# Order of query loads and DMA transposes in one DMA queue, and of the weight formation, in a fused attention and feed-forward kernel

## Chip, cores, metric

One core of one Trainium2 chip. The metric is the device time of one execution in microseconds (us). A run is one execution; every run also lists the mean clock that TensorE was granted, as a share of its full speed.

## The reference

A linear attention (softmax of q over the head dimension, softmax of k over the sequence, two small products) feeds a feed-forward stage.

```python
# q, k, v: (8, 8, 576, 64)   w1, w2: (512, 1024)   w3: (1024, 1024)   w_out: (1024, 512)
q_s = softmax(q, axis=-1);  k_s = softmax(k, axis=2)
kv   = einsum('bhsd,bhse->bhde', k_s, v)
attn = einsum('bhsd,bhde->bhse', q_s, kv)
x    = attn.transpose(0, 2, 1, 3).reshape(4608, 512)
out  = (((x @ w1) * (x @ w2)) @ w3) @ w_out
```

## The kernel before

The kernel folds w3 and w_out into one matrix W3O (the "weight formation"), so that the feed-forward stage is, for each of nine chunks of 512 tokens, a first stage (`s1`, products with w1 and w2) and a second stage (`s2`, product with W3O). The attention of batches 2 to 8 is woven in between. Batches are counted from one in this text; in the code the index is one less.

The parts that matter: every load, DMA transpose (`DMA_TRANSPOSE` in the traces) and output store but the very last is issued by SyncE into one queue, in program order. A query batch goes load, exponential (ScalarE, `eq`), sums (VectorE, `ds`), normalisation (GpSimd, `eqn`), transpose by DMA (`qsT`), product (TensorE, tile `att`), copy to `xT`.

```python
stage = ctx.enter_context(tc.tile_pool(name="stage", bufs=12))   # every load lands here
...
def load_qkv(b, which, i):
    t = slot([P, 2, R * D])                                      # 576 KB
    nc.sync.dma_start(out=t, in_=...)
def dma_t(b, i):
    nc.sync.dma_start_transpose(out=qt_tile(b, i), in_=eqns[(b, i)].rearrange("p r h d -> p (r h d)"))
...
LOADS = [("q", 0), ("q", 1), ("k", 0), ("v", 0), ("k", 1), ("v", 1)]
...
    exp_k(1, 1, 1)
    dma_t(1, 0)                     # second batch's transposes ...
    dma_t(1, 1)
    for which, i in LOADS:          # ... ahead of the third batch's loads
        load_qkv(2, which, i)
...
def step():                         # one step of the attention between two matmul blocks (cut)
    ...
    if b == 2 and n == 9:
        for m in range(6):          # all six loads of the fifth batch, one in each step
            due.setdefault(t + 1 + m, []).append(lambda m=m: load_qkv(4, *LOADS[m]))
    ...
    if n in (2, 5):
        due.setdefault(t + 3, []).append(lambda: dma_t(b, n // 3))
```

In the traces of before and after, the DMAs of the queue name eight completion semaphores in turn, and of the 145 DMAs with an eighth one ahead of them none was issued before that one had landed: the query load issued at 66.06 in the trace of before is the eighth after the key load issued at 55.23, which landed at 66.05. The recorded texts call this queue the ring, and count on landings in the order of issue: in both traces all 154 DMAs landed so.

The softmax here doesn't subtract the row's maximum and nothing guards it: scores larger than these inputs give would overflow.

## Time and profile before

| | before |
|---|---|
| median of 4 runs | 253.57 us (252.31 to 255.34) |
| profiled span | 253.0 us, granted clock 0.986 |
| TensorE (PE) busy | 238.8 us, 94% |

The page of the profile, first its busy line and then three rows of its slices (40 equal slices of 6.3 us; the digit is the busy share in tenths):

```profile
PE 238.8 (94%) x1405; PEld 114.2 (45%) x1405; DVE 129.2 (51%) x235; ACT 110.9 (44%) x190; POOL 66.8 (26%) x63
...
PE   8989999997969978999999999999999999999993
...
PEclk9999999999997997999999999999999999999999
DMA  7999999789899999999799651451111132112335
```

TensorE is full from slice 17 to slice 39; slice 40 is the end. Its weak slices are 10, 12, 15 and 16; the clock is down in the slices 13 and 16, each time with or right after a weak one; and up to there the DMA engines are nearly full, with a shallow hole in slices 8 to 11. The prediction shows the single gaps.

### The profile page before, as it was taken

The numbers are of one execution on the slowest core, as the hardware profiler recorded it, in microseconds if no ns is written. First come the engines' busy times: TensorE is split into PE (matmuls) and PEld (weight loads), VectorE is DVE, ScalarE is ACT, GpSimd is POOL, SyncE is SP. The second block draws the span as 40 slices with busy tenths as digits, with TensorE's granted clock in tenths as the row PEclk, the third lists the DMA queues.
The fourth block names the chain that finished last, engine by engine and source line by source line (L and its number), as shares of the span: only waits on it lengthen the run. The fifth ranks groups of instructions, "written<-read, shape, count | busy, mean of one in ns | idle before, by whom it ended". The sixth has DMA issues, their size and how long they took to land.

```text
span 253.0 us, 3872 instructions
## 1 busy us (share of the span) xinstructions
PE 238.8 (94%) x1405; PEld 114.2 (45%) x1405; DVE 129.2 (51%) x235; ACT 110.9 (44%) x190; POOL 66.8 (26%) x63
## 2 busy tenths in 40 slices
PE   8989999997969978999999999999999999999993
PEld 2534545453424433454454445445444444444442
DVE  2668544757565372546547647635344343444342
ACT  4578515717537615645645563743411222122200
POOL 3655842613621611603503413420000000000000
PEclk9999999999997997999999999999999999999999
DMA  7999999789899999999799651451111132112335
GB/s 243 385 348 367 398 404 391 267 209 383 270 233 373 391 307 374 333 317 396 136 225 370 92 103 39 96 115 41 44 41 41 41 78 49 43 41 58 68 78 131
DMA packets 41875, 52.62 MB, mean 208 GB/s; under 512 B 18816, under 2 KB 22912, under 8 KB 41856
## 3 DMA queue, kind: packets, MB, share of 16 engines
q1 hardware_dynamic: 41776, 52.24, 68.8%
q8 instruction: 11, 0.18, 0.3%
q10 hardware_dynamic: 80, 0.13, 0.1%
q14 instruction: 8, 0.07, 0.1%
HBM read 38.80 MB, written 9.44 MB: 191 GB/s over the span
## 4 chain that ended last, share of the span: by engine, by line
PE 67%; DMA 24%; SPq 4%; DVE 1%; issue 1%; ACT 1%; POOL 0%
PE pab L218 39%; PE po L261 20%; DMA qsT<-eqn 7%; DMA st<-in_moe_w_out_dram 4%; DMA st<-in_k_dram 4%; DMA st<-in_q_dram 4%; DMA st<-in_moe_w_dram 4%; PE att L192 3%; SPq L87 3%; PE pab L261 2%; PE att L154 2%; SPq L77 1%; PE po L302 1%; PE pab L302 1%; DVE osb L263 0%
## 5 line engine op out<-in xcount | busy, mean ns | idle before, releaser
L140 POOL TENSOR_TENSOR eqn<-eq,dr 128x1152 f16<-128x1152 f16 x16 | 34.3, 2146 | 85.4 <-DVE dr L138 60.9
L261 PEld LDWEIGHTS <-abT 128*128 128x128 f16 x296 | 28.7, 98 | 32.3
L263 DVE TENSOR_SCALAR osb<-po 128x512 f32<-128x512 f32 (+1 forms) x32 | 21.7, 679 | 23.3 <-PE po L261 22.2
L133 DVE TENSOR_REDUCE ds<-eq 128x9 f32<-128x576 f16 x32 | 23.6, 744 | 9.1 <-ACT eq L121 9.0
L121 ACT ACTIVATE eq<-st 128x576 f16<-128x576 f32 x32 | 21.1, 684 | 13.1 <-DMA st<-in_q_dram 13.1
L200 ACT CAST xT<-att 128x640 f16<-128x640 f32 (+3 forms) x29 | 17.0, 631 | 17.4 <-PE att L192 17.3
L114 ACT ACTIVATE ek<-st 128x576 f16<-128x576 f32 x32 | 21.0, 683 | 3.8 <-DMA st<-in_k_dram 3.8
L218 PE MATMUL pab<-xT,w_2_81 128*128 128x512 f16 x72 | 18.9, 387 | 0.5 <-ACT a_988 L223 0.5
L218 PE MATMUL pab<-xT,w_2_77 128*128 128x512 f16 x72 | 19.4, 393 | 0.0
L218 PE MATMUL pab<-xT,w_0_75 128*128 128x512 f16 x72 | 18.3, 379 | 1.1 <-ACT xT L200 1.1
L218 PE MATMUL pab<-xT,w_3_78 128*128 128x512 f16 x72 | 19.0, 387 | 0.0
L218 PE MATMUL pab<-xT,w_1_80 128*128 128x512 f16 x72 | 18.5, 379 | 0.2 <-ACT a_902 L223 0.2
L218 PE MATMUL pab<-xT,w_1_76 128*128 128x512 f16 x72 | 18.5, 379 | 0.0
L218 PE MATMUL pab<-xT,w_3_82 128*128 128x512 f16 x72 | 18.5, 379 | 0.0
L218 PE MATMUL pab<-xT,w_0_79 128*128 128x512 f16 x72 | 18.2, 379 | 0.0
L210 PE MATMUL pab<-zero 128*128 128x512 f16 x35 | 11.0, 477 | 1.2 <-DVE zero L319 1.2
L261 PE MATMUL po<-W3O_91,abT 128*128 128x512 f16 (+1 forms) x32 | 12.1, 377 | 0.0
L261 PE MATMUL po<-W3O_94,abT 128*128 128x512 f16 (+1 forms) x32 | 12.0, 376 | 0.0
L261 PE MATMUL po<-W3O_95,abT 128*128 128x512 f16 (+1 forms) x32 | 12.0, 376 | 0.0
L261 PE MATMUL po<-W3O_97,abT 128*128 128x512 f16 (+1 forms) x32 | 12.0, 376 | 0.0
L261 PE MATMUL po<-W3O_98,abT 128*128 128x512 f16 (+1 forms) x32 | 12.0, 376 | 0.0
L261 PE MATMUL po<-W3O_93,abT 128*128 128x512 f16 (+1 forms) x32 | 12.0, 376 | 0.0
(291 smaller groups left out, 350.6 us busy)
## 6 DMA issues: line engine op xcount, KB each, us to landing
st<-in_q_dram SPq DMA_DIRECT2D x16, 576.0 KB, 6.2
st<-in_k_dram SPq DMA_DIRECT2D x16, 576.0 KB, 6.8
st<-in_v_dram SPq DMA_DIRECT2D x16, 576.0 KB, 8.3
out_dram<-osb SPq DMA_DIRECT2D x71, 128.0 KB, 2.4
st<-in_moe_w_dram SPq DMA_DIRECT2D x16, 512.0 KB, 10.5
st<-in_moe_w_out_dram SPq DMA_DIRECT2D x4, 512.0 KB, 11.0
qsT<-eqn SPq DMA_TRANSPOSE x14, 4.3
out_dram<-osb ACTq DMA_DIRECT2D x1, 128.0 KB, 2.6
```

The costliest lines, as they stand in the source:

```text
L87: nc.sync.dma_start(out=t, in_=w.rearrange("(c p) f -> p c f", p=P)[:, :, qt * 256:(qt + 1) * 256])
L114: nc.scalar.activation(out=eks[(b, i)][:, :, hh, :], in_=qkv32[("k", b, i)][:, hh].rearrange("p (r d) -> p r d", r=R), func=AF.Exp)
L121: nc.scalar.activation(out=eqs[(b, i)][:, :, hh, :], in_=qkv32[("q", b, i)][:, hh].rearrange("p (r d) -> p r d", r=R), func=AF.Exp)
L133: nc.vector.tensor_reduce(out=dss[(b, i)][:, :, hh], in_=eqs[(b, i)][:, :, hh, :], axis=AX.X, op=ALU.add)
L140: eng.tensor_tensor(out=eqn.rearrange("p r h d -> p (r h) d"), in0=eqs[(b, i)].rearrange("p r h d -> p (r h) d"), in1=dr[:, :, None].broad ...
L154: nc.tensor.matmul(kvp[:, g, 0:130].rearrange("p (h e) -> p h e", h=2), lhsT=eks[(b, i)][rows, r].rearrange("p h d -> p (h d)"), rhs=v16bu ...
L192: nc.tensor.matmul(xps[g][:, 0:n].rearrange("p (r s) -> p r s", s=SP), lhsT=kv2[:, g, :], rhs=qsT[:, r0:r1, 64 * g:64 * g + 64], start=Tru ...
L200: (copies[0] if copies else nc.scalar.copy)(out=dst, in_=xp[:, :, 0:n])
L210: nc.tensor.matmul(wp, lhsT=zero[:, 0:P], rhs=zero, start=True, stop=True)
L218: nc.tensor.matmul(p, lhsT=wsb[qt][:, ct, fo:fo + P], rhs=xT[:, ct, t0:t0 + CH], start=(ct == 0), stop=(ct == N_CT - 1))
L261: nc.tensor.matmul(po[:, 0:n1 - n0], lhsT=abT[(j, ft)][:, tb * P:(tb + 1) * P], rhs=W3O[ft][:, n0:n1], start=(ft == 0), stop=(ft == N_FT - 1))
L263: nc.vector.tensor_scalar(out=osb[:, n0:n1], in0=po[:, 0:n1 - n0], scalar1=ISC, scalar2=None, op0=ALU.mult)
```

## The change

The intent: the third batch's query loads should not stand behind transposes that wait for GpSimd; the fifth batch's loads should not stand ahead of the fourth's transposes; VectorE should not make TensorE wait in the weight formation. I call the three parts C (queries first), E (fifth batch behind) and A (weight formation).

```diff
# part A
     w3_t(0)
-    s1(0, 7)
     w3_t(1)
     w3_c(3, pcopy, acopy)
+    s1(0, 7)
     w3_t(2)
...
-    ew[0]()
-    ew[1]()
     for ft in range(4, N_FT):
         if ft == 4:
-            w3_c(7, vcopy)
+            w3_c(7, pcopy)
...
             w3_t(ft + 2)
+        for n in {4: (0, 1), 5: (4,)}.get(ft, ()):
+            ew[n]()
         w3_mm(wp, ft, range(4, N_FT))
         nc.scalar.copy(out=W3O[ft], in_=wp)
-        for n in {4: (2, 3, 4), 5: (5, 6), 6: (7,), 7: ()}[ft]:
+        for n in {4: (2, 3), 5: (5, 6), 6: (7,), 7: ()}[ft]:
# part C
+    load_qkv(2, *LOADS[0])
+    load_qkv(2, *LOADS[1])
     dma_t(1, 0)
     dma_t(1, 1)
-    for which, i in LOADS:
+    for which, i in LOADS[2:]:
         load_qkv(2, which, i)
# part E
         if b == 2 and n == 9:
-            for m in range(6):
+            for m in range(2):
                 due.setdefault(t + 1 + m, []).append(lambda m=m: load_qkv(4, *LOADS[m]))
...
+            if b == 3 and n == 5:
+                for m in range(2, 6):
+                    due.setdefault(t + 3 + m // 4, []).append(lambda m=m: load_qkv(4, *LOADS[m]))
```

## The prediction

> **What bounds the kernel now.** I read the page first (PE busy 238.8 of 253.0 us), then the slices: TensorE is full from the eighteenth slice (about 110 us) to the end. So the time is a fixed amount of matmul work plus whatever TensorE loses before 110 us, and nothing after 110 us can be won. Next I read the timeline of TensorE alone, for its gaps:
>
> ```profile
> 44.90 0.62 PE L292 MATMUL att<-ident,w_610 128*128 128x128 f16 x8 [0.84 <-DVE w_610 L280]
> ...
> 61.76 1.02 PE L218 MATMUL pab<-xT,w_0_75 128*128 128x512 f16 x4 [1.05 <-ACT xT L200]
> ...
> 75.25 1.12 PE L192 MATMUL att<-qsT,kvbd_87 128*128 128x320 f16 x4 [1.57 <-DMA qsT<-eqn]
> ...
> 95.58 1.07 PE L192 MATMUL att<-qsT,kvbd_89 128*128 128x320 f16 x4 [2.24 <-DMA qsT<-eqn]
> ```
>
> The bracket is the idle time and what ended it. The same timeline has five smaller gaps: 0.56 at 32.62 (a VectorE copy of a transposed w3 block), 0.49 at 58.98 (an xT copy), 0.18 at 67.28, 0.51 at 72.65 (a16 copies), 0.35 at 76.72 (an xT copy). All nine sum to 7.79 us. Behind the two largest hides a second loss. The busy table of four stretches (columns: PE, weight loads, DVE, ACT, POOL busy us, then clock, DMA share, GB/s):
>
> ```profile
> 71.80:75.20 3.40, 1.37 (x6) 0.35 (x4) 2.70 (x5) 1.28 (x3) 0.71 (x1) 1.00 1.20 239
> 75.20:78.60 3.40, 3.00 (x11) 1.51 (x12) 0.73 (x2) 2.63 (x5) 1.41 (x1) 0.50 1.02 309
> 92.20:95.60 3.40, 1.16 (x7) 0.35 (x5) 1.76 (x4) 0.00 (x0) 1.97 (x1) 1.00 1.32 226
> 95.60:99.00 3.40, 3.40 (x10) 1.40 (x11) 0.00 (x0) 2.37 (x5) 0.15 (x1) 0.51 1.11 359
> ```
>
> After a stretch in which TensorE was busy only 1.37 or 1.16 of 3.40 us, it got half its clock for one stretch: up to 3.4 x 0.5 = 1.7 us lost each time. Who makes the transposed queries qsT late? The chain of waits says DMA:
>
> ```profile
> 55.23 10.82 DMA st<-in_k_dram
> ...
> 69.16 5.95 DMA qsT<-eqn
> ...
> 83.99 11.45 DMA qsT<-eqn
> ```
>
> The columns are start and duration, for a DMA from issue to landing: 11.45 us for a transpose that took 3.3 when issued into an empty queue (48.70). The timeline of the issuing queue shows why:
>
> ```profile
> 48.70 3.89 SPq L180 DMA_TRANSPOSE qsT<-eqn  x2
> 52.65 1.11 SPq L77 DMA_DIRECT2D st<-in_q_dram  x2
> ...
> 83.99 7.19 SPq L180 DMA_TRANSPOSE qsT<-eqn  x1
> ```
>
> The third batch's query loads stand behind the second batch's transposes, which sit waiting for GpSimd until 48.70, although the queue's previous issue was at 38.78. And at 83.99 one transpose holds the queue 7.19 us, having been queued behind seven loads issued from 76.62 to 83.70, four of them the fifth batch's keys and values (batches are counted from one here, as the change does). Last, VectorE and ScalarE:
>
> ```profile
> 43.49 0.76 DVE L133 TENSOR_REDUCE ds<-eq 128x9 f32<-128x576 f16 x1 [1.74 <-ACT eq L121]
> 44.16 0.68 DVE L280 CAST w_610<-st 128x1024 f16<-128x1024 f32 x1
> ```
>
> The cast that TensorE waits for at 44.90 stands on VectorE behind a sum that waited 1.74 us for exponentials of data still in flight.
>
> [...] backlogged 576 KB loads land about 1.5 us apart, which is 589,824 B at the page's 391 to 398 GB/s. [...] So a transpose not ready blocks all behind it, as from 39.41 to 48.70. [...]
>
> **The change, part by part.** No matmul or load is added or removed; only orders change, and one w3 cast moves from VectorE (0.68 us) to GpSimd (1.04).
>
> (a) One first-stage block goes between the w3 transposes. It fills the 0.56 gap at 32.62, but the product after it needs wo_83, whose GpSimd cast ends at 32.74 (landing 32.08), and TensorE began it at 33.06. Gain about 0.3.
>
> (b) Cast w3_7 on GpSimd: its load lands about 41.3 (one 1.3 us step after w_602's, 40.0), GpSimd is free at 41.15, so it is ready at 42.4, and TensorE comes for it at about 43.6. Gap gone: 0.84. W3O_98's copy now follows an exponential of keys landing at 48.75, which may return 0.1. Lead at the second stage: about 1.1 us (48.6 rather than 49.7). The sums also run without the casts between, so the second batch's eqn is ready near 47.4 rather than 48.7.
>
> (c) Query loads of batch 3 first. The last load before them lands at 38.78 + 11.4 = 50.1. In ring order the two land at 51.6 and 53.1, rather than 57.0 (52.65 + 4.4) and 60.4 (53.27 + 7.1). ScalarE waited 5.49 us for the first at 57.09, and VectorE's sums then delayed the xT copies; with the data there, the gaps 0.49 and 1.05 close to about 0.1: gain 1.4. Price: the second batch's transposes now land behind the loads, about 54.3 and 55.3; TensorE needs the first at 56.11 - 1.1 - 0.1 = 54.9. Just in time.
>
> (d) Everything behind moves up. k and v of batch 3 are issued from about 53.3 instead of 53.80, but with two loads (3 us) fewer ahead: the last lands near 64 instead of 67.4. That lets batch 4's queries be issued near 61.8 and 64 (66.06 and 67.49), and batch 3's transposes follow: about 70.3 to 71.1 for the first, 1 us more for the second, instead of 75.11. TensorE, ahead by 1.1 + 1.4 + 0.2 + 0.35 (most of the 0.51 a16 gap) = 3.05, arrives at 75.25 - 1.57 - 3.05 = 70.6. So the 1.57 + 0.35 = 1.92 us of gap shrink to about 1.2 (0.5 for the second transpose and the copy included). [...] I count the half-clock stretch as gone: 1.4 (what its matmuls ran over, 4 x 1.51 against 1.03 and so on, less than the 1.7 ceiling). Gain 0.55 + 0.7 + 1.4 = 2.65.
>
> (e) Fifth batch's k and v behind the fourth's transposes. In front of the fourth batch's first transpose remain four loads of its own batch and three query loads; in ring order it lands near 85, its partner near 88. TensorE, ahead by 1.1 + 1.4 + 2.65 = 5.15, needs them at 93.34 - 5.15 = 88.2 and about 92. Both in time: 2.24 of gap and about 1.7 of half clock go: 3.95. The loads pushed back are first read at 102.74 (before), about 93.6 in the new time; issued from about 85, when the second transpose has been taken up, and with 4.2 us for the first (as for the load at 74.07) and 1.5 for each more, they land from about 89.4 to 94, four steps ahead of its use.
>
> Sum: 1.1 + 1.4 + 2.65 + 3.95 = 9.1. From 253.56: 244.5. I add 0.3 for small new waits: **244.8 us**.
>
> **Rivals.** *The transposes become the late part*: (c) puts two loads before the first pair with 0.6 us to spare. One late load there costs 1 to 2 us of TensorE and perhaps a half-clock stretch: 247 to 248. For it: landings of 57.01, then 60.36 show a 1.85 us slip. Against: that slip came after the time in question. *The third batch's transposes stay late*: then (d) yields only 1 and the half clock at 75 stays: about 246.5. For it: my slack there is negative by a few tenths. *The DMA queue is simply full*, and a TensorE 9 us ahead runs into later transposes. Against: the fifth batch's first transpose landed at 109.3 (101.14 + 8.2) and was used at 116.75; busy DMA falls to half or less after 127 us; I keep 3 us of slack. If true: 248. *Nothing moves*, because the gaps are swallowed by PSUM buffers held by ScalarE and VectorE: against it, both are busy under 60% in these stretches.
>
> **Range and chances.** All rivals but the last are partial losses, so the range is lopsided: 242.3 (all of (d) too) to 248.8. Runs of before spread by 3 us, another reason for width. Faster by over 2% means below 248.5: 0.88. Within 2%: 0.11. Slower: 0.01.
>
> **What would show it.** Right: no gap at w3_7's transposes; ScalarE's eq after 50 us without DMA wait; the qsT gaps near 70 at about 1 us, none near 88; no 0.50 clock stretch between 60 and 110 us; TensorE's full stretch starting about 9 us earlier. Wrong: a DMA-ended gap at the second batch's qsT (about 55), a half-clock stretch kept, or gaps after 110 us. The figure fails if landings in the ring are not in order, or if the half clock needs far less idle than I assume.

## The result

| | before | after |
|---|---|---|
| median of 4 runs | 253.57 us (252.31 to 255.34) | 246.68 us (245.62 to 247.6) |
| profiled span | 253.0 us, clock 0.986 | 244.2 us, clock 1.0 |
| ratio | | 0.9722, 95% interval 0.9646 to 0.9798 |

Ratios here are the mean time of one kernel's fast runs over that of the other's of the same rounds, so not quite the ratio of the medians. A run over 1.5% above the fastest of its kernel in its call is called slow and left out of the ratios: 257.42 and 255.55 us of before and 253.71 us of e2. The runs of one call share a chip and the runs of the kernel before; only compare times of one call with each other.

The same rows of the page of the changed kernel (slices of 6.1 us):

```profile
PE 235.1 (96%) x1405; PEld 113.3 (46%) x1405; DVE 128.5 (53%) x234; ACT 111.0 (45%) x190; POOL 68.2 (28%) x64
...
PE   8989999999969999999999999999999999999993
...
PEclk9999999999999999999999999999999999999999
DMA  6999999999999999999999514411213222123235
```

One weak slice is left, the twelfth, and no slice has a lowered clock; DMA has no hole in slices 8 to 11 any more. The timeline of TensorE has these gaps after 30 us, and no other:

```profile
32.62 1.46 PE L302 MATMUL pab<-wo_83,qsT 128*128 128x512 f16 x6 [0.26 <-POOL wo_83 L286]
71.49 0.65 PE L192 MATMUL att<-qsT,kvbd_87 128*128 128x320 f16 x4 [1.73 <-DMA qsT<-eqn]
72.70 0.87 PE L192 MATMUL att<-qsT,kvbd_88 128*128 128x320 f16 x4 [0.56 <-ACT xT L200]
```

So 2.55 us of gaps instead of 7.79. The wait for the third batch's transpose is left; it is even a little longer than before (1.57). The timeline of the queue (start, duration of issue) shows parts C and E:

```profile
38.60 0.53 SPq L77 DMA_DIRECT2D st<-in_v_dram  x1
40.01 2.60 SPq L77 DMA_DIRECT2D st<-in_q_dram  x2
47.51 5.78 SPq L180 DMA_TRANSPOSE qsT<-eqn  x2
...
74.41 7.26 SPq L180 DMA_TRANSPOSE qsT<-eqn  x1
```

The queries are issued at 40.01 instead of 52.65, and the fourth batch's first transpose at 74.41 instead of 83.99. It still holds the queue for 7.26 us (7.19 before), but starts 9.6 us earlier. What released ScalarE's first exponential of the third batch's queries (timeline of ScalarE), and the link in the chain of waits before the remaining gap:

```profile
51.80 1.26 ACT L121 ACTIVATE eq<-st 128x576 f16<-128x576 f32 x2 [0.71 <-DMA st<-in_q_dram]
```

```profile
65.30 6.06 DMA qsT<-eqn
```

The wait of 5.49 us became 0.71, and these exponentials run 5.3 us earlier. The transpose that TensorE waits for was issued at 65.30 and landed 6.06 us later, at 71.4.

**Half-clock stretches.** The busy table around the remaining gap of the changed kernel:

```profile
68.10:71.50 3.40, 1.67 (x8) 0.53 (x7) 2.49 (x5) 1.17 (x3) 0.93 (x1) 1.00 1.23 240
```

TensorE is busy 1.67 of 3.40 us there, and in this run no half-clock stretch follows. But the four runs of the changed kernel are of two kinds: 245.62 and 245.97 us at clock 1.0, 247.38 and 247.6 us at clock 0.993. In the trace of before the clock is 0.50 from 75.18 to 78.59 and from 95.66 to 99.07, 3.41 us each time. One such stretch in a span of 245 us makes the mean clock 1 - 0.5 x 3.41 / 245 = 0.993, and costs, as an estimate, up to 0.5 x 3.41 = 1.7 us. So I take the mean clock of a run to count its half-clock stretches: 1.0 none, 0.993 one, 0.986 two; the traces of before (two, 0.986) and of the changed kernel (none, 1.0) agree. Values from 0.996 to 0.999 are less than one such stretch: 0.996 is 2.0 us at half clock by the same arithmetic, an estimate. The trace of before shows a fall that takes nothing from TensorE: from 252.67 us to the end of the span at 252.98 the clock is 0.50, and the last product ended at 248.93. This is used below.

### The profile page after: what moved, and what is told of

It is laid out like the page before. It is cut to its first block, busy times and chain, and to the rows that moved or that the text cites. A ratio compares the mean times of both kernels' runs of the same rounds, so it can differ in the third digit from the quotient of the medians.

```text
span 244.2 us, 3871 instructions
## 1 busy us (share of the span) xinstructions
PE 235.1 (96%) x1405; PEld 113.3 (46%) x1405; DVE 128.5 (53%) x234; ACT 111.0 (45%) x190; POOL 68.2 (28%) x64
## 3 DMA queue, kind: packets, MB, share of 16 engines
q1 hardware_dynamic: 41776, 52.24, 71.1%
## 4 chain that ended last, share of the span: by engine, by line
PE 74%; DMA 19%; DVE 2%; SPq 1%; ACT 1%; issue 1%; POOL 1%; DVEq 0%
PE pab L218 41%; PE po L261 22%; DMA st<-in_moe_w_dram 8%; DMA st<-in_k_dram 5%; PE pab L210 4%; DMA out_dram<-osb 3%; PE att L154 3%; PE att L192 3%; DMA qsT<-eqn 2%; PE pab L261 2%; SPq L77 1%; POOL w_3_82 L94 1%; PE att L175 0%; DVE osb L263 0%; SPq L267 0%
## 5 line engine op out<-in xcount | busy, mean ns | idle before, releaser
L218 PE MATMUL pab<-xT,w_1_80 128*128 128x512 f16 x72 | 18.5, 379 | 0.0
L218 PE MATMUL pab<-xT,w_1_76 128*128 128x512 f16 x72 | 18.5, 379 | 0.0
L218 PE MATMUL pab<-xT,w_2_77 128*128 128x512 f16 x72 | 18.5, 379 | 0.0
L218 PE MATMUL pab<-xT,w_3_78 128*128 128x512 f16 x72 | 18.5, 379 | 0.0
L218 PE MATMUL pab<-xT,w_3_82 128*128 128x512 f16 x72 | 18.5, 379 | 0.0
L218 PE MATMUL pab<-xT,w_2_81 128*128 128x512 f16 x72 | 18.5, 379 | 0.0
L218 PE MATMUL pab<-xT,w_0_75 128*128 128x512 f16 x72 | 18.3, 379 | 0.0
L218 PE MATMUL pab<-xT,w_0_79 128*128 128x512 f16 x72 | 18.2, 379 | 0.0
L261 PE MATMUL po<-W3O_91,abT 128*128 128x512 f16 (+1 forms) x32 | 12.0, 376 | 0.0
L261 PE MATMUL po<-W3O_95,abT 128*128 128x512 f16 (+1 forms) x32 | 12.0, 376 | 0.0
L261 PE MATMUL po<-W3O_97,abT 128*128 128x512 f16 (+1 forms) x32 | 12.0, 376 | 0.0
L261 PE MATMUL po<-W3O_93,abT 128*128 128x512 f16 (+1 forms) x32 | 12.0, 376 | 0.0
L261 PE MATMUL po<-W3O_94,abT 128*128 128x512 f16 (+1 forms) x32 | 12.0, 376 | 0.0
L261 PE MATMUL po<-W3O_96,abT 128*128 128x512 f16 (+1 forms) x32 | 12.0, 376 | 0.0
L261 PE MATMUL po<-W3O_98,abT 128*128 128x512 f16 (+1 forms) x32 | 12.0, 376 | 0.0
```

What stands on the lines that cost most here:

```text
L218: nc.tensor.matmul(p, lhsT=wsb[qt][:, ct, fo:fo + P], rhs=xT[:, ct, t0:t0 + CH], start=(ct == 0), stop=(ct == N_CT - 1))
L261: nc.tensor.matmul(po[:, 0:n1 - n0], lhsT=abT[(j, ft)][:, tb * P:(tb + 1) * P], rhs=W3O[ft][:, n0:n1], start=(ft == 0), stop=(ft == N_FT - 1))
```

## The experiments

Four kernels ran in each call, beside the kernel before (11 runs in each call, medians 254.91, 253.94 and 253.66 us). All results were correct.

| run | what it is | median us | ratio to before, 95% interval |
|---|---|---|---|
| e1 | A alone | 253.13 | 0.9919, 0.9884 to 0.9955 |
| e2 | C alone | 252.14 | 0.9909, 0.9869 to 0.995 |
| e3 | E alone | 249.13 | 0.9791, 0.9753 to 0.9829 |
| e4 | C and E | 246.37 | 0.9678, 0.9642 to 0.9715 |
| e5 | A, C and E (the change) | 245.87 | 0.9696, 0.9652 to 0.974 |
| e6 | change, stores held back | 246.39 | 0.9715, 0.9672 to 0.9758 |
| e7 | change, one query load later | 244.77 | 0.9651, 0.9613 to 0.9689 |
| e8 | e6 and e7 | 248.65 | 0.9795, 0.9745 to 0.9845 |
| e9 | change, stores behind the keys | 244.48 | 0.9662, 0.9612 to 0.9712 |
| e10 | e7 without A | 246.14 | 0.9717, 0.9674 to 0.9761 |
| e11 | e7 again | 245.75 | 0.9692, 0.9646 to 0.9737 |
| e12 | A and C | 251.13 | 0.9901, 0.9847 to 0.9955 |

e1 to e4 were one call, e5 to e8 the second, e9 to e12 the third. Two theories are tested. **Mine:** the end is set, gap by gap, by when a transpose lands, and that is set by what the queue must work off ahead of it; time won elsewhere is waited away there. **The rival:** each gap is a loss of its own, and the parts add.

### e1: part A alone

```diff
 (the kernel before, with part A of the change)
+        for n in {4: (0, 1), 5: (4,)}.get(ft, ()):
+            ew[n]()
...
```

> Only the weight formation's new order (part a and b), loads as before. My theory: the gaps 0.56 at 32.6 and 0.84 at 44.9 shrink to 0.26 and 0; eqn of the second batch is ready about 1.3 us earlier, so its transposes and everything queued behind them move up by about 1.3 us too. All later gaps stay, both qsT gaps (1.6 and 2.2 us) with their half-clock stretches included. Ratio to before 0.995 (about 1.2 us). Rival (gaps add up and the queue does not move with the weights): TensorE arrives 1.1 us earlier and waits 1.1 us longer at the qsT of the third batch, ratio 1.000.

Measured 0.9919, 2.1 us. I expected 1.2, which the interval takes in; the rival, nothing, which it does not. The queue did move with the weights, and by more than I said: the third batch's first transpose landed at 72.1 in this trace (75.1 before), the fourth's at 92.8 (95.4). TensorE's wait for the latter grew, from 2.24 us (its timeline):

```profile
92.92 1.12 PE L192 MATMUL att<-qsT,kvbd 128*128 128x320 f16 x4 [3.57 <-DMA qsT<-eqn]
```

So the end moved with the landing, by 2.9 us between the two profiles (253.0 and 250.1) where the landing moved 2.7, and the rest was waited away.

### e2: part C alone

```diff
 (the kernel before)
+    load_qkv(2, *LOADS[0])
+    load_qkv(2, *LOADS[1])
     dma_t(1, 0)
     dma_t(1, 1)
-    for which, i in LOADS:
+    for which, i in LOADS[2:]:
         load_qkv(2, which, i)
```

> Only the third batch's two query loads ahead of the second batch's transposes. My theory: the gaps 0.49 and 1.05 near 60 and 0.18, 0.51 near 70 close; the third batch's first transpose lands at about 71.4 as in the changed kernel (75.1 before), TensorE needs it at about 71.6, so that gap is under 0.5 us. But the fourth batch's transposes stay behind seven loads that only move up with the queue, about 3.5 us, so the wait near 90 GROWS from 2.2 to about 3.7 us with a half-clock stretch, and the end moves by no more than the queue moved: 3.5 us, ratio 0.986. Rival (each gap is a loss by itself, so the parts add): 5 us, ratio 0.980.

Measured 0.9909, 2.3 us: less than my 3.5, whose ratio of 0.986 lies just outside the interval, and far from the rival's 0.980. The four gaps near 60 and 70 closed as expected. The third batch's transpose landed at 71.7 in the profile, but TensorE waited 1.05 us there, not under 0.5, and a half-clock stretch followed. The fourth's landed at 92.1, where the queue's move put it:

```profile
92.28 0.65 PE L192 MATMUL att<-qsT,kvbd 128*128 128x320 f16 x4 [1.61 <-DMA qsT<-eqn]
```

The wait did not grow, since TensorE came later than I reckoned; the end moved with the landing all the same. From this landing to the end of the span are 157.6 us in the profile of before (95.44 to 253.0), 157.3 in e1 and 157.4 in e12, each with a half-clock stretch behind the landing, and 155.9 here, where none followed it. The profiled run was the fastest of six (249.78 us); of the six, two had two half-clock stretches, one of them the run left out as slow.

### e3: part E alone

```diff
 (the kernel before)
-            for m in range(6):
+            for m in range(2):
...
+            if b == 3 and n == 5:
+                for m in range(2, 6):
+                    due.setdefault(t + 3 + m // 4, []).append(lambda m=m: load_qkv(4, *LOADS[m]))
```

> Only the fifth batch's keys and values moved behind the fourth's transposes. My theory: everything to 90 us as before, including the qsT gap at 75 with its half clock; the 2.24 us gap at 95.6 and the half-clock stretch after it vanish, since four loads (6 us in ring order) fewer stand ahead of the transpose: about 3.9 us, ratio 0.985. Rival (transposes are late for another reason than the loads queued ahead): the gap stays, ratio 1.000.

Measured 0.9791: 5.3 us where I expected 3.9, whose ratio of 0.985 lies outside the interval. The gap near 95 is gone, as expected, and so is the stretch behind it: no run had two half-clock stretches, and four of six had none (0.997 to 1.0). In the kernel before, not one of the 33 runs beside the experiments had none: 19 had one (0.991 to 0.993), 14 had two. So, by inference, since only a trace shows where a stretch lies, the stretch behind the fourth batch's transpose came in nearly every run and the one at 75 us in somewhat under half of them. Between the two profiles the span fell by 4.0 us, as expected, though the profiled run of e3 is its slowest; why the medians fell by a further 1.3 us or so I cannot say.

### e4: without part A

```diff
 (the changed kernel, part A undone)
-            w3_c(7, pcopy)
+            w3_c(7, vcopy)
...
```

> The whole change except the weight formation's order. My theory: the third batch's first transpose lands when the ring has worked off what is ahead of it, about 71.4, whatever TensorE does; so the 1.1 us that the weight formation wins is only waited away there. Without it TensorE arrives 1.1 us later, the gap of 1.73 us shrinks to about 0.6, the half-clock stretch is rarer, and the time equals that of the whole change: ratio to before 0.968 to 0.974, median 245.5 to 247. Rival (parts add): 1.1 us slower than the whole change, median about 247.8, ratio 0.977.

Measured 0.9678, the changed kernel 0.9696: part A, worth 2.1 us alone, is worth nothing measurable on top of C and E (the two intervals, each about 1 us wide to either side, leave room for a few tenths). The time is what I expected, and the rival's 0.977 is outside the interval. The detail is not: in the profiled run the gap was

```profile
72.23 0.65 PE L192 MATMUL att<-qsT,kvbd 128*128 128x320 f16 x4 [1.58 <-DMA qsT<-eqn]
```

and not 0.6, because the transpose landed 0.75 us later than in the profile of the changed kernel (72.10 against 71.35). That run had a half-clock stretch; it was the slowest of the six, and the only one with a stretch.

### e5: the changed kernel again

No edit.

> The changed kernel once more, beside the runs that follow. Theory: the two kinds of run seen at first return: clock 1.0 near 245.8 us, and clock 0.993 (one half-clock stretch after the wait for the third batch's transpose) about 1.7 us above. Mean against the kernel before 0.967 to 0.973. Rival (the two kinds were chance): no relation between clock and time.

Five runs had clocks of 0.998 to 1.0 and took 244.87 to 246.49 us; one had 0.993 and took 247.6. With the four runs of the first result that is seven without a stretch, mean 245.7, and three with one, mean 247.5. The difference is 1.8 us. A stretch alone costs at most 1.7 by the estimate above, so a longer wait ahead of it is probably in this figure too. The two kinds of run are thus real, but which one comes is not the kernel's doing alone. In this profile the transpose landed at 70.57 and the gap was only 0.56 us.

### e6: the first chunk's stores held back

```diff
-    s2(0, 0, alt=True)
+    held = []
+    s2(0, 0, alt=True, hold=held)      # and the same for s2(0, 1), s2(0, 2), s2(0, 3)
...
             due.setdefault(t + 3, []).append(lambda: dma_t(b, n // 3))
+            if b == 2 and n == 5:
+                due[t + 3].append(lambda: [put() for put in held])
```

> The changed kernel with the eight output stores of the first chunk issued after the third batch's second transpose, instead of six ahead of batch 4's queries and two ahead of the first transpose. Theory (the transpose is late because of what the ring must work off ahead of it): eight stores are about 2 us of ring, and the two query loads are issued near 56 instead of 62 to 64 since they no longer wait for the eighth transfer before them; so the transpose lands near 68.5 instead of 71.4, the 1.73 us gap is gone, the 0.56 copy gap may stay, clock 1.0 in nearly all runs: median 1.7 to 2.7 us under the changed kernel of the same call. Rival (the transpose is late because it waits for its input eqn, or by a fixed latency after issue): it lands at 71.4 as before, same time.

A miss in the time: mean 246.46 us against 245.98 for e5. The step that I tested held: the transpose landed at 68.97 and its gap is gone, so the queue's content was what made it late, and not its input. But the queue then looked like this:

```profile
59.29 8.01 SPq L180 DMA_TRANSPOSE qsT<-eqn  x2
67.42 5.04 SPq L268 DMA_DIRECT2D out_dram<-osb  x8
72.56 1.47 SPq L77 DMA_DIRECT2D st<-in_k_dram  x1
```

Issuing the eight stores took SyncE 5.04 us, and the fourth batch's keys behind them were issued at 72.56 instead of 70.30. ScalarE waited 2.78 us for them, its copy for the first stage came late, and TensorE stood still elsewhere:

```profile
79.33 1.02 PE L218 MATMUL pab<-xT,w 128*128 128x512 f16 x4 [1.73 <-ACT a L223]
```

By chance the same 1.73 us, in a new place. No run of e6 had a half-clock stretch (0.998 to 1.0).

### e7: one query load behind the transposes

```diff
-                for m in range(2, 6):
+                for m in range(1, 6):
                     due[t + 3].append(lambda m=m: load_qkv(3, *LOADS[m]))
...
     load_qkv(3, *LOADS[0])
-    load_qkv(3, *LOADS[1])
```

> The changed kernel with only the second of the fourth batch's two query loads moved behind the third batch's transposes. Theory: one load fewer (1.5 us of ring, 2.5 us in landings of the trace) ahead: the transpose lands near 69.4, gap at most 0.3, clock 1.0 in nearly all runs. The moved load lands near 72, about when ScalarE wants it, so it may cost a few tenths: median 1 to 2 us under the changed kernel. Rival: as in the run before, no difference; second rival: ScalarE waits over 1 us for the moved queries and a new gap of 0.5 to 1 us appears near 75, eating half the gain.

Mean 244.77 us against 245.98 of e5: 1.2 us faster, and no run with a half-clock stretch (0.997 to 1.0). The transpose landed at 68.77. The gaps left in the timeline of TensorE after 30 us:

```profile
70.71 0.87 PE L192 MATMUL att<-qsT,kvbd 128*128 128x320 f16 x4 [0.56 <-ACT xT L200]
74.38 4.48 PE L218 MATMUL pab<-xT,w 128*128 128x512 f16 x20 [0.21 <-ACT a L223]
```

The second is the price of the later load, 0.21 us here and 0.86 in the profile of e11, the same kernel run again. There the gain on the changed kernel did not repeat (see e11).

### e8: both moves

```diff
 (the edits of e6 and of e7)
```

> Both moves together. Theory: the transposes land near 67, well before TensorE comes (69.8), so the second move adds nothing to the stores' move: same median as with the stores alone within 0.5 us. If the parts added like independent losses it would be over 1 us faster than the better of the two.

A plain miss: median 248.65 us, 2.5 us slower than e5 by the means (248.49 and 245.98). The transposes did land at 65.7 and 66.9, in good time. But the moved query load now stood behind the eight stores, was issued at 70.36 and landed at 74.60. ScalarE waited for it for 3.86 us, with its copies for the first stage behind it (timeline of ScalarE):

```profile
74.69 0.68 ACT L121 ACTIVATE eq<-st 128x576 f16<-128x576 f32 x1 [3.86 <-DMA st<-in_q_dram]
```

and TensorE behind ScalarE for 3.21 us at 77.06. Four of six runs had a lowered clock again (0.986 to 0.993).

### e9: the stores behind the keys and values

```diff
 (e6, but the held stores are put out after the fourth batch's keys and values)
                     due[t + 3].append(lambda m=m: load_qkv(3, *LOADS[m]))
+                due[t + 3].append(lambda: [put() for put in held])
```

> The changed kernel with the eight stores of the first chunk issued after the fourth batch's keys and values, not between them and the transposes. Theory: holding the stores back was right for the transpose and wrong for the loads behind it: eight stores of 0.57 us of issue each delayed the keys' issue from 70.3 to 72.6[...], which gave the 1.73 us wait of TensorE near 79. With the loads first, the keys are issued near 67.5 and land by 73.5, the gap near 79 is gone, only the 0.56 copy gap stays: median 244.2 to 245.2, within 0.5 us of the kernel with one query load moved. Rival (holding the stores costs something else, output buffers for instance): gap of over 1 us after 75, median 246 or more.

As expected: median 244.48 us, no half-clock stretch, keys issued at 66.60 (timeline of the queue):

```profile
66.60 0.51 SPq L77 DMA_DIRECT2D st<-in_k_dram  x1
...
68.70 7.36 SPq L268 DMA_DIRECT2D out_dram<-osb  x8
```

The gap of 1.73 us is gone, so the place of the stores was its cause. Near 70 only the copy gap of 0.56 is left, and 0.28 at a transpose near 87. It is 0.8 us under e11 by the means (244.72 and 245.49), which the scatter of the runs, up to 2.3 us within one kernel, does not settle.

### e10 and e11: part A where no transpose is late

```diff
 (e10: the edit of e7, with part A undone; e11: e7 unchanged)
```

> The kernel with one query load moved, but with the weight formation's order of before. Theory: where no transpose makes TensorE wait near 70, the 1.1 us of the weight formation are no longer waited away, so this is 0.7 to 1.3 us slower than the next run. Rival (the new weight order is worth nothing by itself): equal within 0.3 us.

> The kernel with one query load moved, once more as the standard for the other two: ratio to before 0.962 to 0.968, clock at least 0.997 in every run.

e11 came out at 0.9692, above the 0.962 to 0.968 that I gave, with clocks as expected. It is no better than the changed kernel was in e5 (0.9696), so the 1.2 us by which e7 beat e5 are not established. Part A is worth 0.65 us here by the means (246.14 and 245.49), 1.3 us between the two profiles (244.4 and 243.1), against a scatter of about 2 us within each kernel. That leans to my theory and does not prove it. The profile of e11 also has the 0.86 us wait for the moved query load, and that of e10, where TensorE comes later, does not have it: the next wait takes part of the gain again.

### e12: without part E

```diff
 (the changed kernel, part E undone)
-            for m in range(2):
+            for m in range(6):
...
```

> The whole change except that the fifth batch's loads stay where they were. Theory: the end is set by the landing of the fourth batch's first transpose, which stands behind seven loads and only moves with the queue: near 92 as with the query loads alone (92.14); TensorE, earlier by the weights' 1.1 us, only waits longer there (2.5 to 3.5 us, half clock after it in most runs). Ratio to before 0.986 to 0.992, as the query loads alone. Rival (parts add): 0.983 or less.

Measured 0.9901, as C alone (0.9909) and not the 0.983 of the parts added. The fourth batch's first transpose landed at 92.57 (e2: 92.14), and TensorE waited for it:

```profile
92.70 1.12 PE L192 MATMUL att<-qsT,kvbd 128*128 128x320 f16 x4 [2.62 <-DMA qsT<-eqn]
```

## Why the prediction was right, and where a size was off

The measured median lies inside the range, and the direction and the chance fit. Point by point:

- **(a) and (b), weights.** The gap at 32.62 is 0.26 us, as worked out; the gap at w3_7's transposes is gone. The second stage began at 48.22 (48.6 predicted), 0.3 of the difference being a head start, see (d). W3O_98's copy costs 0.27 us (its first product starts 0.49 us after the one before, not 0.22), where 0.1 was foreseen.
- **(c), queries first.** The trace of the changed kernel has the two landings at 51.72 and 53.22 (predicted 51.6, 53.1), the second batch's transposes at 54.33 and 55.92 (54.3, 55.3), and no wait for them. The two gaps near 60 are gone entirely.
- **(d), everything moves up.** Batch 4's queries were issued at 62.05 and 63.58 (61.8, 64). The third batch's transpose landed at 71.35, at the late end of 70.3 to 71.1 and beyond. The gap of 1.92 us was to shrink to 1.2 and became 1.73 + 0.56 = 2.29. **This term was mis-sized by 1.1 us.** It has two halves. TensorE came at 69.8 (71.49 - 1.73), 0.8 us before the 70.6 foreseen, 0.3 of it because this run was that much ahead in the untouched beginning (the product that starts at 13.71 in the timeline of before starts at 13.42). And the landing was 0.65 us behind the middle of what I gave. What came early was only waited away. e6, e7 and e9 show the cause: the transpose is late by what stands ahead of it in the queue, stores and query loads. That was the mechanism as predicted; the size was off. In e5's profile, the same kernel, the landing at 70.57 left a gap of 0.56.
- **(e), fifth batch behind.** Landings 86.05 and 88.50 (85, 88), no gap, and the fifth batch's first key landed at 90.0 (89.4). e12 shows that this part is needed for the rest to count.
- **The half clock.** I counted two stretches, 1.4 and 1.7 us, as removed; that the shorter wait in (d) would bring none was my estimate. The profile of before had two, but most of its runs (19 of 33) had one; and the changed kernel keeps one in three of its ten runs, because the gap in (d) was left: the 30 runs of e6, e7, e9, e10 and e11, whose traces show no wait for a transpose near 70 us, have none (0.996 to 1.0). In stretches that is about 1.4 less 0.3 = 1.1 removed instead of 2; 0.9 at up to 1.7 us each is, as an estimate, **up to 1.5 us less**. This was the other mis-sized term.

The two profiled runs show the sum nearly as I had it: 253.0 to 244.2 is 8.8 us, against 9.1. That it is so close is partly luck: the gaps shrank by 5.2 us (7.79 to 2.55) where I counted 6.0 (1.1, 1.4, 1.25 and 2.24), and TensorE's busy time fell by 3.7 us where I counted 3.1 for the half clock. The medians fell by 6.9 us only. The profiled run of before took 254.76 us, 1.2 above the median from which I subtracted, and that of after 245.97, 0.7 below its median; these two make up the 1.9 us between 244.8 and 246.68. So the step that was off is that I took from a median what one profiled run had lost, two half-clock stretches among it; by the estimate above these are most of the 1.9 us.

Three readings in the prediction do not hold, though its sum does not use them. On the page of before the DMA engines are at half or less from about 145 us on and not from 127: slices 21 and 22 (126 to 139 us) still show 9. And VectorE and ScalarE are not both under 60% busy in the four stretches shown: 2.70 of 3.40 us (79%) for VectorE in the first, 2.63 (77%) for ScalarE in the second. The queue into which the transpose was issued at 48.70 was not empty: two loads landed after that, at 48.75 and 50.14, before the transpose at 52.04. "The page's 391 to 398 GB/s" there are figures of the profile's page.

The first rival (the second batch's transposes become late) did not come. The second (the third batch's stay late) did in part: the gap stayed, the half clock mostly not. The third (the DMA queue is simply full) did not: the changed kernel has no gap after 73 us. The last rival, that nothing moves, fell.

**What stayed of the gain's parts.** Alone, A, C and E win 0.81, 0.91 and 2.09% of the time; together 3.04% in e5, not 3.81%. C and E add (3.22% in e4); A is waited away at the next late transpose, with C (e12) as with C and E (e4). Part E is the largest: without it the other two end at the same late landing. With it, the end follows the third batch's landing instead. From that landing to the end of the span are 172.8 us in the profiles of the changed kernel (71.35 to 244.2) and of e5 (70.57 to 243.4), and 174.3 in e3 (74.70 to 249.0) and e4 (72.10 to 246.4), which have a half-clock stretch behind it.

**What stays open.** Why e3 won about 1.3 us more than its gap and its stretch; what idle time brings the half clock; and whether the landings that slip by 1 to 2 us do so because of the packets that the page counts as `instruction` (q8: 11 packets, 0.18 MB). In time some slips fall together with such a packet (57.01 to 60.36 in the trace of before, 57.65 to 60.51 in that of the changed kernel), and the one that counts most does not: the query load ahead of the transpose of (d) landed at 69.44, 2.6 us after its partner, and no such packet lies between the two.

**A version that may beat both.** e7 was 1.2 us (0.5%) faster than the changed kernel, but run again (e11) it was only level with it by the ratio to before; e9, at 0.9662, lies between e7 (0.9651) and e11 (0.9692). No run of e7, e9 or e11 had a half-clock stretch, against three of ten of the changed kernel. That either is faster is not shown.

## What to carry to other kernels

Where one queue carries loads, transposes and stores, take each waited-for transfer and ask what stands ahead of it: here a transpose whose input was not ready held back all behind it (SyncE issued nothing from 39.41 to 48.70 in the kernel before), and a load needed later delayed a transpose too (one load less ahead: 68.77 instead of 70.57). What was moved out of the way came into another's way (TensorE then waited 1.73 us elsewhere in e6, 3.21 us in e8), so follow the queue until every transfer is ahead of its first use. A gain upstream of a wait that something else sets is worth nothing until that wait is gone; and count half-clock stretches over many runs, not in one profile (the changed kernel had one in three of ten runs).

## What the traces showed of the clock and the queue

- **Idle time before the half clock.** In the trace of before, waits of 1.57 and 2.24 us were followed by it. In eight cases over six traces (before, e1 to e4, e12, mean clocks 0.985 to 0.993) the half clock followed a stretch of 3.41 us in which TensorE was busy for 0.26 to 1.75 us; in e2 the longest gap was 1.05 us, with 0.56 soon after, and the busy table says

```profile
70.49:73.90 3.41, 1.75 (x11) 0.89 (x10) 1.00 (x3) 1.65 (x4) 2.12 (x1) 1.00 1.10 251
```

  The length of the longest gap alone does not decide: in the trace of e8 (mean clock 1.0) a gap of 3.21 us was followed by no half clock. Nor does the busy time of just any stretch of that length: the changed kernel was busy for 1.67 of 3.40 us (68.10 to 71.50), less than in e2, and had a clock of 1.00 there and in the 3.40 us after. What decides is not shown; the same kernel had a stretch in three of ten runs.
- **Issue of a transpose.** After 122 us of the trace of before, with two or three DMAs outstanding, issuing one took SyncE 1.29 to 1.39 us each; with seven loads outstanding (changed kernel, 74.41) it took 7.26 us, during which SyncE issued nothing else.
- **Order of landing.** In the traces of before and after none of the 154 DMAs landed before one issued earlier, and backlogged loads of 576 KB landed about 1.5 us apart (85.44, 86.94, 88.44, 89.92 in the trace of before).
- **Instruction packets.** In the trace of before one packet of kind `instruction` (q8, 0.02 MB) lies between 57.0 and 60.3 us, and the load then landing came 3.4 us after its predecessor (57.0, 60.4) instead of 1.5. This is a coincidence in time, and not shown as a cause: in the changed kernel one such packet lies in the late landing from 57.65 to 60.51, and none in those from 66.87 to 69.44, 78.08 to 80.45 and 96.15 to 99.01.
